# A Fourier and expert-mixing kernel on one core: the identity table loaded first, one product group per chunk, output products in quads over eight banks

## The chip, the cores and the metric

The kernel runs on one core of a Trainium2 chip. The metric is the device time of one execution in microseconds (us). The engines are named as in the profile: PE is the matrix engine (PEld its weight loads), DVE the vector engine, ACT the scalar engine, POOL the third elementwise engine, SP the engine that issues the transfers. PE's results land in PSUM, which has eight banks of 128 x 512 fp32; everything else lies in SBUF.

## The reference, cut to what matters

```python
X = np.fft.fft(np.fft.fft(x, axis=1), axis=2)      # x: 8 x 2496 x 256, fp32
x = X.real.reshape(8 * 2496, 256)                  # 19968 tokens
logits = x @ phi                                   # 32 slots, 8 experts x 4
d = np.exp(logits - logits.max(0)); d /= d.sum(0) + 1e-9
slot_input = d.T @ x                               # 32 x 256
for e in range(8):                                 # 4 slots each, F = 1024
    slot_out[e] = np.maximum(slot_input[e] @ w1[e], 0) @ w2[e]
c = np.exp(logits - logits.max(1, keepdims=True)); c /= c.sum(1, keepdims=True) + 1e-9
return c @ slot_out                                # 19968 x 256
```

## The kernel before, in words

The transformed tokens are never formed. The transform is linear, so the slots' table is transformed instead (`phi_`, `phv`), and the sequence's 2496 points are taken as 39 x 64. The eight sequences make five units: units 0 and 1 are one sequence each (two tiles of x), units 2 to 4 two sequences each (four tiles). A tile is 128 partitions of ten rows of 256 fp32, 1280 KB (1152 KB for the first tile of a two-sequence unit), and is loaded by `lx` into one of four buffers `raw`.

For each tile, `nf` adds the mirrored half (L349, mostly on POOL), `es` copies a half into PSUM (ACT) and `ef` writes sums and differences into a buffer `eo` (two DVE instructions, L365 and L366). Only then is the `raw` buffer free for the next load. Units 0 to 2 go on through PE: `pt` transposes against the identity (L379), `yt` copies the result out of PSUM into `xt`, and `zp` multiplies a chunk of ten rows by the slots' table (L410) in two groups, of four rows (128 columns) and of six (192 columns). Units 3 and 4 use DVE's 32 x 32 transpose (`xt`) and `zv` (L442) instead. Then, for each unit: `tz` (DVE transpose, L462), the 64-point product `am` (L482), the 39-point product `cm` (L503), the slots' maxima, the exponentials `xp`, the transform back (`em`, `dm`) and the product `um` with the kept `eo` tiles, which frees these for pieces of the weights (`lw`). When all units are done their sums are merged (`sl` to `si`), `hm` (L745) and `vm` (L779) apply the experts, and `rm`, `rc` make `rh`, the slots' outputs repeated on the four groups of 32 partitions.

The last stage makes the output. For each pair p of sequences a softmax over the slots (`x1` to `x6`) gives `hl`, and `om` multiplies 32 rows of `rh` by 32 rows of `hl`: five blocks b per pair, each with four row groups g, so 80 banks in all. Blocks 0 to 3 take one product of 512 columns for each g, block 4 two of 224. `oe` copies a bank into an output buffer (L907, ACT or DVE), and `st` stores a block of four banks (1024 KB, or 896 KB for block 4). In the trace every fp32 product is two MATMUL records, each with its weight load; transposes are one.

The order of the work is written out by hand in `ORDER`, a list of some 800 names such as `om.0.2.1`. Each engine, SP too, runs its instructions strictly in that order. PSUM banks and buffers are handed out in this order as well: `bank` takes the bank that was released first. The kernel before uses six banks this way; the other two hold `stage`, `ubank` and `mini` (maxima and sums).

Of the kernel before, what the change touches and what calls it, by code (L numbers as in the profile page):

```python
# [40 lines left out]
lx.3.1 am.0.1 tz.1.0.0 pt.2.0.2 es.2.2 nf.2.3.G cm_.0.0 ao.0.1.A ef.2.2.V yt.2.0.2.A pt.2.0.4 cm_.0.1
yt.2.0.4.A pt.2.0.3 mr.0.1 lx.3.2 lc_.0.0.A zp.2.0.0 mr.0.0 nf.3.0.G es.2.3 lc_.0.1.V cf.0.0 mt.0 pt.2.1.1
cf.0.1 yt.2.0.3.A ef.2.3.V pt.2.1.0 zp.2.0.1 yt.2.1.0.A mn.0 es.3.0 lx.3.3 pt.2.1.2 tz.1.0.1 nf.3.1.G pt.2.1.4
mw.0.A yt.2.1.1.A ef.3.0.V mb.0 pt.2.1.3 yt.2.1.2.A am.1.0 mq.0.A xp.0.0 tz.2.0.0 yt.2.1.4.A lx.4.0 phv xp.0.1
xt.3.0 yt.2.1.3.A nf.3.2.G es.3.1 zp.2.1.0 xp.0.4 ef.3.1.V am.1.1 ao.1.0.A zp.2.1.1 ao.1.1.A xp.0.3 xp.0.2
cm_.1.0 tz.2.0.1 lx.4.2 lw.17 xp.0.6 nf.3.3.G xp.0.5 tz.2.1.1 xp.0.7 cm_.1.1 xp.0.8 em.0.0 xp.0.9 tz.2.1.0
es.3.2 mr.1.0 am.2.1 xp.0.10 ec.0.0.A mr.1.1 nf.4.0.G xt.3.1 em.0.1 ao.2.1.A am.2.0 ec.0.1.A phw.A dm.0.0.0
ef.3.2.V mt.1 dc.0.0.0.A zv.3.0 ao.2.0.A mn.1 lx.4.1 es.3.3 xt.3.2 lc_.1.0.A mw.1.A ef.3.3.V dm.0.0.1 cm_.2.0
dc.0.0.1.A tz.3.0.0 cm_.2.1 lx.4.3 lc_.2.0.A xt.3.3 es.4.0 mb.1 am.2.2 um.0.0 nf.4.1.G ao.2.2.A mr.2.0 mq.1.A
lc_.2.1.A lc_.1.1.V cf.2.0 zv.3.1 mr.2.1 xp.1.0 xp.1.4 ef.4.0.V xp.1.8 cf.2.1 xp.1.3 xp.1.1 nf.4.2.G xp.1.10  # L50
xp.1.2 tz.3.0.1 xp.1.7 lw.6 lk.2 xp.1.6 tk.0 cm_.2.2 xp.1.5 tz.3.1.1 tc_.0.A xp.1.9 ct.0.0 es.4.1 tz.3.1.0
em.1.0 nf.4.3.G cc.0.0.A ef.4.1.V am.3.0 ec.1.0.A mr.2.2 lw.8 am.3.1 ao.3.0.A xt.4.0 es.4.2 em.1.1 mt.2
lc_.2.2.A cm_.3.0 ao.3.1.A ec.1.1.V cf.2.2 cf.1.0 cf.1.1 ef.4.2.V dm.1.0.0 am.3.2 dm.1.0.1 lc_.3.0.V lw.9
ao.3.2.A ct.0.1 es.4.3 mn.2 mr.3.0 cm_.3.2 dc.1.0.0.A uc.0.V cf.3.0 cm_.3.1 dc.1.0.1.A mw.2.V cc.0.1.V mb.2
ct.0.2 xt.4.1 mq.2.A um.1.0 xp.2.4 xp.2.8 xp.2.0 mr.3.2 xp.2.5 zv.4.0 xp.2.3 lw.3 lc_.3.2.V lc_.3.1.A ef.4.3.V
xp.2.9 xp.2.10 xp.2.2 xp.2.1 mr.3.1 lw.7 tk.1 em.2.0 xt.4.2 tc_.1.A cf.3.1 cf.3.2 xp.2.7 xp.2.6 mt.3 ec.2.0.A
em.2.1 mn.3 uc.1.A xt.4.3 mw.3.A em.2.2 ec.2.1.A dm.2.0.0 tz.4.0.0 ec.2.2.A mb.3 cc.0.2.A zv.4.1 tz.4.0.1
# [110 lines left out]
def _build(nc, tc, xh, phih, w1h, w2h, cins, where, out):  # L168
# [4 lines left out]
    with ctx:  # L173
# [228 lines left out]
        def zp(_, u, c, q):  # L402
# [11 lines left out]
            if q:  # L414
                drop(("et", u, c))
# [586 lines left out]
```

## Time and profile before

| what | value |
|---|---|
| median of 3 runs | 201.61 us (201.05 to 202.61) |
| the profiled execution | 200.02 us, span 198.2 us from first to last instruction |
[...]
| busy share of the span | PE 84%, PEld 56%, DVE 64%, ACT 47%, POOL 26% |
| moved by DMA | 59.15 MB, of these 20.45 MB written |

The busy time of PE counts records whose ends are modelled, so 84% isn't 84% of what it could do. A transfer is "issued" when SP hands it over and "landed" when its semaphore rises.

### The profile page before, as it was taken

The page shows a single profiled execution, that of the slowest core. Times are in us where ns is not written, and L with a number is a line of the kernel's source. Part 1 is how long each engine was busy: PE and PEld are TensorE (multiplying, and loading weights), DVE is VectorE, ACT ScalarE, POOL GpSimd, SP SyncE. Part 2 cuts the span into 40 slices and gives each one's busy share as a digit, 9 for nine tenths or more (in the row PEclk, how much of TensorE's full clock was granted, in tenths as well). Part 3 has the DMA queues.
Part 4 walks back from the last instruction along what each step waited for, and adds up shares of the span by engine and source line. Part 5 has one row for each costly group of instructions (what it writes and reads, how often), then busy time and mean ns, then how long its engine had stood idle before and what let it go on. Part 6 is the DMA issues. An engine that isn't in the chain of part 4 may idle for free.

```text
span 198.2 us, 5688 instructions
## 1 busy us (share of the span) xinstructions
PE 166.0 (84%) x2454; PEld 110.1 (56%) x2454; DVE 126.3 (64%) x209; ACT 93.1 (47%) x219; POOL 50.9 (26%) x35
## 2 busy tenths in 40 slices
PE   0006999884999998999999999989999989999920
PEld 0006887673755565667767875465456566756500
DVE  0753975980696995998938897999717532245420
ACT  0032637760664754786615642557645345421130
POOL 0046787879004920002000231006020000000000
PEclk9999999997999999999999999999999955555555
DMA  6999999899249398850089999402989998769865
GB/s 223 424 422 427 421 420 395 306 405 347 110 140 386 82 403 297 268 237 3 3 310 399 435 408 355 172 3 91 390 362 375 383 413 332 291 279 382 332 258 245
DMA packets 8952, 59.15 MB, mean 298 GB/s; under 512 B 1120, under 2 KB 1120, under 8 KB 4192
## 3 DMA queue, kind: packets, MB, share of 16 engines
q1 hardware_dynamic: 8928, 58.80, 75.3%
q8 instruction: 19, 0.31, 0.6%
q14 instruction: 5, 0.04, 0.1%
HBM read 38.35 MB, written 20.45 MB: 297 GB/s over the span
## 4 chain that ended last, share of the span: by engine, by line
PE 58%; DVE 4%; ACT 1%; issue 1%; ACTq 0%
PE psum L895 25%; PE psum L442 4%; PE psum L584 4%; PE psum L779 4%; PE psum L641 4%; PE psum L745 4%; PE psum L614 3%; PE psum L482 3%; PE psum L503 3%; PE psum L816 2%; DVE acc L697 1%; ACT raw L907 1%; DVE cm L861 1%; DVE es L601 1%; PE psum L800 0%
## 5 line engine op out<-in xcount | busy, mean ns | idle before, releaser
L349 POOL TENSOR_TENSOR raw<-raw 128x1280 f32<-128x1280 f32 (+1 forms) x14 | 39.0, 2794 | 30.5 <-DMA raw<-xh 18.1
L907 ACT COPY raw<-psum 128x512 f32<-128x512 f32 (+1 forms) x46 | 24.2, 587 | 29.7 <-PE psum L895 29.6
L907 DVE COPY raw<-psum 128x512 f32<-128x512 f32 (+1 forms) x34 | 21.6, 665 | 23.2 <-PE psum L895 23.0
L895 PE MATMUL psum<-ds,rh 32*128 32x512 f32 (+1 forms) x96 | 34.4, 748 | 0.6 <-ACT raw L907 0.6
L895 PE MATMUL psum<-es,rh 32*128 32x512 f32 (+1 forms) x96 | 30.9, 693 | 0.7 <-ACT rh L805 0.4
L379 PE MATMUL psum<-cs,eo 128*128 128x128 f32 x80 | 12.2, 302 | 16.5 <-DMA cs<-c 16.5
L895 PEld LDWEIGHTS psum<-ds,rh 32*128 32x128 f32 x96 | 18.3, 256 | 9.5 <-DVE raw L907 3.3
L895 PEld LDWEIGHTS psum<-es,rh 32*128 32x128 f32 x96 | 15.2, 235 | 9.4 <-ACT raw L907 3.8
L379 PEld LDWEIGHTS psum<-cs,eo 128*128 128x128 f32 x80 | 10.2, 157 | 18.0 <-issue 17.8
L462 DVE STREAM_TRANSPOSE zt<-psum 128x320 f32<-128x320 f32 x16 | 12.5, 836 | 10.0 <-PE psum L410 8.7
L574 ACT ACTIVATE d<-lt,nm 120x128 f32<-120x128 f32 (+1 forms) x55 | 16.5, 372 | 0.1
L365 DVE TENSOR_TENSOR eo<-raw,psum 128x640 f32<-128x640 f32 x15 | 12.1, 809 | 4.6 <-ACT psum L354 4.4
L410 PE MATMUL psum<-xt,wphi 128*32 128x128 f32 (+1 forms) x192 | 12.1, 317 | 3.2 <-issue 3.2
L354 ACT COPY psum<-raw 128x640 f32<-128x640 f32 x15 | 10.6, 705 | 6.8 <-POOL raw L349 6.2
L482 PE MATMUL psum<-cs,zt 128*64 128x64 f32 x352 | 13.2, 227 | 0.7 <-issue 0.7
L482 PEld LDWEIGHTS psum<-cs,zt 128*64 128x64 f32 x352 | 11.8, 141 | 2.5 <-issue 2.1
L584 PE MATMUL psum<-cs,d 120*64 120x60 f32 x352 | 12.2, 223 | 0.0
L584 PEld LDWEIGHTS psum<-cs,d 120*64 120x64 f32 x352 | 11.4, 138 | 1.4 <-issue 0.2
L366 DVE TENSOR_TENSOR eo<-raw,psum 128x640 f32<-128x640 f32 x15 | 12.1, 809 | 0.0
L495 ACT COPY o<-psum 124x512 f32<-124x512 f32 (+2 forms) x12 | 6.2, 524 | 12.2 <-PE psum L482 11.0
L423 DVE STREAM_TRANSPOSE xt<-eo 128x1280 f32<-128x1280 f32 x8 | 11.9, 1489 | 0.0
L387 ACT COPY xt<-psum 128x512 f32<-128x512 f32 x16 | 9.0, 589 | 6.2 <-PE psum L379 6.2
(129 smaller groups left out, 238.2 us busy)
## 6 DMA issues: line engine op xcount, KB each, us to landing
raw<-xh SPq DMA_DIRECT2D x13, 1280.0 KB, 7.5
out<-raw SPq DMA_DIRECT2D x15, 1024.0 KB, 4.7
eo<-w2h SPq DMA_DIRECT2D x12, 640.0 KB, 8.3
raw<-w1h SPq DMA_DIRECT2D x4, 1280.0 KB, 7.2
out<-raw SPq DMA_DIRECT2D x4, 896.0 KB, 4.0
raw<-xh SPq DMA_DIRECT2D x3, 1152.0 KB, 8.3
xt<-w1h SPq DMA_DIRECT2D x2, 1280.0 KB, 9.2
eo<-w1h SPq DMA_DIRECT2D x1, 512.0 KB, 3.6
```

What stands on the lines that cost most here:

```text
L349: (v if e == "V" else gp).tensor_tensor(a, a, b, op=ALU.add)
L365: en.tensor_tensor(b[:, :, 0:128], x[:, :, 0:128], y, op=ALU.add)
L366: en.tensor_tensor(b[:, :, 128:256], x[:, :, 0:128], y, op=ALU.subtract)
L379: pe.transpose(b[:, o : o + 128], T["eo", u, 2 * c + r // 5][:, r % 5, k * 128 : k * 128 + 128], C("ident"))
L410: pe.matmul(z[h][32 * g : 32 * g + 32, r0 : r0 + n], wphi[:, w], x[:, :, h, 32 * ah : 32 * ah + 32], start=i != 1, stop=i != 0, tile_posit ...
L423: v.transpose(T["xt", u, t // 2][:, 5 * (t % 2) : 5 * (t % 2) + 5].rearrange("p r n -> p (r n)"), T["eo", u, t].rearrange("p r d -> p (r d)"),
L462: v.transpose(dst, T["z", u, c][h])
L482: pe.matmul(ps[64 * r : 64 * r + 64, 64 * j : 64 * j + 64], T["zt", u][:, o : o + 64], C("wa0")[:, 64 * r : 64 * r + 64], start=True, stop ...
L574: sc.activation(d, src, AF.Exp, bias=nm[:, u % 2, i : i + 1], scale=1.0)
L584: pe.matmul(ps[64 * r : 64 * r + 64, 60 * j : 60 * j + 60], T["d", u, b][:120, 64 * j : 64 * j + 64], C(f"etab{r}"), start=True, stop=True ...
L895: pe.matmul(ps[:, j * w : j * w + w], rh[rows, 128 * dc : 128 * dc + 128], T["hl", p][rows, 32 * r0 : 32 * r0 + w], start=True, stop=True, ...
L907: COPY[e](T["ot", p, b][:, g * w : g * w + w], T["po", p, b, g][:, :w])
```

## The change

The tables are cut differently: the identity (64 KB) is a table of its own, transfer `lk.1`, and the other tables come behind it (`lk.2`, `lk.3`). The first tile of x is loaded as two pieces (two rows of each half, then three), with `nf` and `ef` in two pieces too. `zp` makes one group of 320 columns. `om` makes all four row groups of a block in one go, each in a bank of its own, and `rel`, run when the merging is done, gives the last two banks to the pool. `ini` clears `zt`'s padding once and runs one exponential. `rh` moves into a buffer `o1`. `ORDER` is rewritten throughout: among others `phv` moves from the middle of unit 2 to before the first `zp`, and one more `nf` runs on DVE. Operations `zq`, `zc` and a table `wq` are added for a kind of unit that isn't used.

```diff
@@ ORDER, its first and some of its last lines
-ini lx.0.0 lx.0.1 lx.1.0 lx.1.1 lk.1 lk.0 nf.0.0.V ef.0.0.V nf.0.1.V lx.2.0 es.0.1 ef.0.1.V nf.1.0.G lx.2.1
+ini lx.0.0.0.2 lx.0.1 lk.0 lk.1 nf.0.0.0.2.V lx.0.0.2.5 lx.1.0 lx.1.1 ef.0.0.0.2.V nf.0.1.V pt.0.0.0 phi_
...
-om.3.3.0 oe.2.3.3.V om.3.1.3 om.3.4.3 st.2.3.0.4 oe.3.4.0.V oe.3.1.3.V om.3.3.1 oe.3.4.3.V st.3.1.0.4 om.3.3.2
+om.2.4 oe.3.4.0.A oe.3.4.1.V oe.3.4.2.A oe.3.4.3.A oe.2.4.0.V om.3.3 st.3.4.0.4 oe.2.4.1.V oe.2.4.2.A
@@
+    unit = [("ident", np.eye(128))]
     zero = [
-        ("ident", np.eye(128)),
...
-    for group in (first, zero, late):
+    for group in (first, unit, zero, late):
@@
+        def more():
+            banks.extend([psum[:, 3072:3584], psum[:, 3584:4096]])
+            idle.extend([6, 7])
@@ lx
-        def lx(_, u, t):
+        def lx(_, u, t, a=0, b=0):
...
+            if b:
+                sy.dma_start(
+                    x.rearrange("p (m r) d -> p m r d", m=2)[:, :, a:b],
+                    xh[:, r0 * D : (r0 + 10) * D].rearrange("p (m r d) -> p m r d", m=2, d=D)[:, :, a:b],
+                )
+                return
@@ ini
+            gp.memset(sm[:, 39:40], 0.0)
+            sc.activation(sm[:, 39:40], sm[:, 39:40], AF.Exp)
             gp.memset(wphi[:, 1], 0.0)
+            for z in homes["zt"]:
+                gp.memset(z[:, 640:664], 0.0)
+                gp.memset(z[:, 1300:1324], 0.0)
@@ zp
-        ZR = ((0, 4), (4, 6))
-        def zp(_, u, c, q):
-            z = zbanks(u, c) if q == 0 else T["z", u, c]
-            r0, n = ZR[q]
+        def zp(_, u, c):
+            z = zbanks(u, c)
...
-                            z[h][32 * g : 32 * g + 32, r0 : r0 + n], wphi[:, w], x[:, :, h, 32 * ah : 32 * ah + 32],
+                            z[h][32 * g : 32 * g + 32], wphi[:, w], x[:, :, h, 32 * ah : 32 * ah + 32],
@@ rc
-            COPY[e](rh[:, 128 * dh : 128 * dh + 128], T["rm", dh][:, :128])
+            if dh == 0:
+                T["rh"] = home("rh", "o1")
+            COPY[e](T["rh"][:, 128 * dh : 128 * dh + 128], T["rm", dh][:, :128])
@@ om
+        def rel(_):
+            more()
-        def om(_, p, b, g):
-            ps = bank(("po", p, b, g))
-            T["po", p, b, g] = ps
-            rows = slice(32 * g, 32 * g + 32)
+        def om(_, p, b):
...
+            for g in range(4):
+                T["po", p, b, g] = bank(("po", p, b, g))
             for j, dc in enumerate(dcs):
+                for g in range(4):
+                    rows = slice(32 * g, 32 * g + 32)
+                    pe.matmul(
+                        T["po", p, b, g][:, j * w : j * w + w], T["rh"][rows, 128 * dc : 128 * dc + 128],
+                        T["hl", p][rows, 32 * r0 : 32 * r0 + w],
+                        start=True, stop=True, tile_position=(32 * g, 0),
+                    )
```

On SP at the start, before (`raw` are the four buffers of x, `c` and `phih` the tables; here the tables that hold the identity are `cs_98`):

```order
L267 DMA raw_61<-xh 128x2560
L267 DMA raw_62<-xh 128x2560
L267 DMA raw_63<-xh 128x2560
L267 DMA raw_64<-xh 128x2560
L256 DMA cs_98<-c 128x626
L253 DMA eo_65<-c 128x544
L254 DMA phi<-phih 128x64
L267 DMA raw_61<-xh 128x2304
```

and on SP at the start now (`cs_98` is the identity alone, `cs_99` the tables of the 64- and 39-point products):

```order
L272 DMA raw_61<-xh 128x2x512
L277 DMA raw_62<-xh 128x2560
L253 DMA eo_65<-c 128x544
L254 DMA phi<-phih 128x64
L256 DMA cs_98<-c 128x128
L272 DMA raw_61<-xh 128x2x768
L277 DMA raw_63<-xh 128x2560
L277 DMA raw_64<-xh 128x2560
L277 DMA raw_62<-xh 128x2304
L256 DMA cs_99<-c 128x498
```

The identity stood behind four whole tiles of x; now it stands behind one and two fifths of a tile, and the other tables behind five tiles.

On PE from unit 2's last chunk on, before (L410 is `zp`, L328 `phv`, L482 `am`):

```order
L410 MATMUL psum<-xt_79,wphi 32x192 x12
L379 MATMUL psum<-cs_98,eo_72 128x128 x2
L379 MATMUL psum<-cs_98,eo_73 128x128 x6
L554 MATMUL psum<-cs_98,mex 120x11
L379 MATMUL psum<-cs_98,eo_73 128x128 x4
L482 MATMUL psum<-cs_98,zt_86 64x64 x16
L328 MATMUL psum<-phi,eo_65 32x32 x72
L410 MATMUL psum<-xt_80,wphi 32x128 x12
L482 MATMUL psum<-cs_98,zt_86 64x64 x6
```

and on PE from its first instruction now (L405 is `pt`, L316 and L318 `phi_`, L350 `phv`, L431 `zp`, L531 `am`):

```order
L405 MATMUL psum<-cs_98,eo_66 128x128 x4
L316 MATMUL psum<-phi,eo_65 128x32 x4
L318 MATMUL psum<-phi,eo_65 1x32 x2
L405 MATMUL psum<-cs_98,eo_67 128x128 x8
L405 MATMUL psum<-cs_98,eo_66 128x128 x2
L405 MATMUL psum<-cs_98,eo_67 128x128 x2
L405 MATMUL psum<-cs_98,eo_66 128x128 x4
L350 MATMUL psum<-phi,eo_65 32x32 x72
L431 MATMUL psum<-xt_79,wphi 32x320 x12
L405 MATMUL psum<-cs_98,eo_68 128x128 x8
L531 MATMUL psum<-cs_99,zt_85 64x64 x22
```

The 72 small products of `phv` went from behind unit 1's second `am` to a place before the first `zp`, with only 26 PE products ahead of them.

On PE in the output stage, before (`es` and `ds` hold `hl` of the pairs, L895 is `om`):

```order
L895 MATMUL psum<-ds_90,rh 128x512
L895 MATMUL psum<-ds_90,rh 128x224 x2
L895 MATMUL psum<-ds_90,rh 128x512
L895 MATMUL psum<-es_87,rh 128x512
L895 MATMUL psum<-es_88,rh 128x512
L895 MATMUL psum<-es_88,rh 128x224 x2
L895 MATMUL psum<-es_88,rh 128x512 x2
L895 MATMUL psum<-es_87,rh 128x512
```

and on PE in the output stage now (`o_92` is `rh`, L952 is `om`):

```order
L952 MATMUL psum<-es_87,o_92 128x224 x8
L952 MATMUL psum<-es_87,o_92 128x512 x8
L952 MATMUL psum<-ds_90,o_92 128x512 x8
L952 MATMUL psum<-es_88,o_92 128x512 x4
L952 MATMUL psum<-ds_89,o_92 128x224 x8
L952 MATMUL psum<-ds_90,o_92 128x224 x8
```

Products of two or three blocks alternated, one row group at a time; now the four row groups of a block stand together.

## Rows read from the trace of the kernel before

**Rows 1.** The page, part 2: granted clock and DMA in 40 equal slices.
```profile
PEclk9999999997999999999999999999999955555555
DMA  6999999899249398850089999402989998769865
GB/s 223 424 422 427 421 420 395 306 405 347 110 140 386 82 403 297 268 237 3 3 310 399 435 408 355 172 3 91 390 362 375 383 413 332 291 279 382 332 258 245
```

**Rows 2.** Busy time by stretch; last three columns granted clock, DMA share, GB/s.
```profile
16.50:62.46 45.96, 41.27 (x719) 30.55 (x719) 32.72 (x48) 24.22 (x55) 27.38 (x17) 0.96 0.85 328
...
47.30:50.30 3.00, 3.00 (x30) 2.01 (x31) 0.00 (x0) 1.05 (x5) 2.45 (x3) 0.51 0.97 394
...
62.46:111.25 48.79, 48.07 (x1033) 33.55 (x1035) 39.02 (x66) 29.76 (x88) 10.37 (x7) 1.00 0.65 241
111.25:133.10 21.85, 21.06 (x388) 13.24 (x382) 19.36 (x42) 10.71 (x25) 3.52 (x3) 1.00 0.68 268
...
150.00:159.20 9.20, 8.64 (x48) 5.01 (x47) 5.15 (x9) 4.80 (x10) 0.00 (x0) 1.00 0.97 402
159.20:190.00 30.80, 30.05 (x92) 19.02 (x92) 12.53 (x20) 9.62 (x19) 0.00 (x0) 0.50 0.82 336
```

**Rows 3.** Timeline, the first 17 us: start, duration, engine, line; idle before in brackets.
```profile
6.35 1.49 DVE L349 TENSOR_TENSOR raw<-raw 128x1280 f32<-128x1280 f32 x1 [6.35 <-DMA raw<-xh]
...
16.50 4.27 PE L379 MATMUL psum<-cs,eo 128*128 128x128 f32 x24 [16.50 <-DMA cs<-c]
```

**Rows 4.** Timeline around PE's stop at 44 us.
```profile
41.81 1.40 PE L328 MATMUL psum<-phi,eo 128*32 128x32 f32 x142
...
47.28 1.08 PE L410 MATMUL psum<-xt,wphi 128*32 128x128 f32 x10 [3.21 <-issue]
...
51.26 1.51 DVE L462 STREAM_TRANSPOSE zt<-psum 128x320 f32<-128x320 f32 x2 [6.33 <-PE psum L410]
...
56.40 3.82 SPq L267 DMA_DIRECT2D raw<-xh  x2
```

**Rows 5.** Waits on SP's queue: total us, times, longest.
```profile
SPq L267 <- DVE eo L366: 48.6, 12, 11.3
```

**Rows 6.** DMA: instruction queue (packets, MB), bytes of the span, issues of x.
```profile
q8 instruction: 19, 0.31, 0.6%
...
HBM read 38.35 MB, written 20.45 MB: 297 GB/s over the span
...
raw<-xh SPq DMA_DIRECT2D x13, 1280.0 KB, 7.5
...
raw<-xh SPq DMA_DIRECT2D x3, 1152.0 KB, 8.3
```

**Rows 7.** The chain that ended last, in order of time: start, us, what.
```profile
64.81 2.82 PE psum L442 x72
...
102.92 1.70 PE psum L503 x4
...
127.48 1.72 PE psum L745 x16
...
133.12 4.79 PE psum L895 x21
...
159.20 15.54 PE psum L895 x37
```

**Rows 8.** Timeline: the two groups of unit 0's product.
```profile
22.92 1.10 PE L410 MATMUL psum<-xt,wphi 128*32 128x128 f32 x24
...
24.54 1.53 PE L410 MATMUL psum<-xt,wphi 128*32 128x192 f32 x24
```

**Rows 9.** Groups of instructions from 133 us on: busy us, mean ns, idle before.
```profile
L907 ACT COPY raw<-psum 128x512 f32<-128x512 f32 x39 | 21.4, 595 | 24.5 <-PE psum L895 24.4
...
L907 DVE COPY raw<-psum 128x512 f32<-128x512 f32 x25 | 16.5, 680 | 15.2 <-PE psum L895 15.1
```

**Rows 10.** Timeline of SP's queue: the stores.
```profile
136.60 54.95 SPq L913 DMA_DIRECT2D out<-raw  x22
```

More of the change, by code (lines that the diff above doesn't have):

```diff
@@ L41 @@
[L41 to L45, printed above, removed]
@@ L312, in phc @@
             v.tensor_copy(wphi[:1, 1], ps[:1, 32:64])
+            if any(f == "Q" for _, _, f in UNITS):
+                for k in range(2):
+                    v.tensor_copy(wq[:, k, 0], ps[:, 0:32])
+                    v.tensor_scalar(wq[:, k, 1], ps[:, 64:96], 1.0 - 2 * k, None, op0=ALU.mult)
+                    v.tensor_tensor(
+                        wq[:1, k, 0], wphi[:1, 0], ps[:1, 32:64], op=ALU.subtract if k else ALU.add
+                    )
             release("phi")
@@ L344, in nf @@
         @op
-        def nf(e, u, t):
-            lo = 1 if t == 0 and not single(u) else 0
+        def nf(e, u, t, r0=0, r1=5):
+            lo = first(u, t)
             x = T["x", u, t]
-            a, b = (x[:, 2:6], x[:, 6:10]) if lo else (x[:, 0:5], x[:, 5:10])
+            a, b = (x[:, 2:6], x[:, 6:10]) if lo else (x[:, r0:r1], x[:, 5 + r0 : 5 + r1])
             (v if e == "V" else gp).tensor_tensor(a, a, b, op=ALU.add)
@@ L352, in es @@
         def es(_, u, t):
-            lo = 1 if t == 0 and not single(u) else 0
+            lo = first(u, t)
             sc.copy(stage, T["x", u, t][:, lo : lo + 5, 128:256])
@@ L357, in ef @@
         @op
-        def ef(e, u, t):
-            lo = 1 if t == 0 and not single(u) else 0
-            x = T["x", u, t][:, lo : lo + 5]
-            b = home(("eo", u, t), "eo").rearrange("p (r d) -> p r d", d=D)
-            T["eo", u, t] = b
+        def ef(e, u, t, r0=0, r1=5):
+            lo = first(u, t)
+            x = T["x", u, t][:, lo + r0 : lo + r1]
+            if r0 == 0:
+                T["eo", u, t] = home(("eo", u, t), "eo").rearrange("p (r d) -> p r d", d=D)
+            b = T["eo", u, t][:, r0:r1]
             en = v if e == "V" else gp
@@ L366, in ef @@
             en.tensor_tensor(b[:, :, 128:256], x[:, :, 0:128], y, op=ALU.subtract)
[L367 removed]
+            if r1 == 5:
+                drop(("x", u, t))
         @op
@@ L903, in oe @@
             w = 512 if b < 4 else 448
-            if g == 0:
-                kind = next(k for k in OT if free[k])
-                T["ot", p, b] = home(("ot", p, b), kind)
+            if ("ot", p, b) not in T:
+                T["ot", p, b] = home(("ot", p, b), next(k for k in OT if free[k]))
             COPY[e](T["ot", p, b][:, g * w : g * w + w], T["po", p, b, g][:, :w])
```

158 lines of the change are left out of this document (91 added, 67 removed).

## The prediction

> **What bounds the kernel now.** I read the slices first. [...]
>
> The **input** begins with a wait. PE's first product starts at 16.50 us, released by the tables that hold the identity, although the first tile of x was there at 6.35 [rows 3]. Later PE stops for 3.21 us without any wait that the profile names, and this right after `phv`'s 142 records in 1.40 us [rows 4]; after it the clock is 0.51 for 3 us [rows 2]. DVE, strictly in order, then waits 6.33 us for `zp`, so that `ef` frees no buffer, and SP holds the next load of x for 11.3 us [rows 4, 5]. The last two tiles are issued at 56.4 and 59.9 us instead of a few us behind the others. In the **middle** the chain runs through PE from 62 to 111 us without a pause worth naming (48.07 of 48.79 us busy), with DVE at 39.02 of 48.79 behind it [rows 2]. From 111.25 to 133.1 the merging and the experts follow, one after the other. In the **output** PE is busy, ACT and DVE wait for it (24.4 and 15.1 us, [rows 9]), and the DMA stands at 0.97 only from 150 to 159 us; from 159.2, with the clock at half, it falls to 0.82 [rows 2]. There the bound is PE's own pace: 37 records in 15.54 us [rows 7].
>
> **The output stage.** A record of 512 columns that has the array to itself takes 1.70 / 4 = 0.43 us (`cm`). `hm`, whose four column groups follow each other in the program, makes 16 such records in 1.72 us, 0.11 each: four abreast. `om` before needs 4.79 / 21 = 0.23 us at the full clock and 15.54 / 37 = 0.42 at half [rows 7]: two abreast in both, since neighbours in the program often share a row group or wait for a bank. Quads put four different row groups and four banks side by side. If they run four abreast, a block of eight records takes 8 x 0.11 = 0.86 us, and 1.72 at the half clock; if only two abreast, 1.8 and 3.4 us. No row of before shows a quad of row groups; the nearest, `zv` (four row groups and two to four column groups), makes 72 records of 320 columns in 2.82 us, where alone each would take 0.43 x 320 / 512 = 0.27: nearly seven abreast. I take four abreast, and 3.4 us for the other end.
>
> Then the stores are late next. 20.45 MB are written [rows 6]; at the 402 GB/s of 150 to 159 us [rows 2] that is 50.9 us, or 2.6 us for each of 20 blocks, longer than the 1.72 of PE. Before, first `om` to the end took 198.2 - 133.1 = 65.1 us: 3.5 until the first store [rows 10], then a stream with holes. Now: 3.0 until the first store, 50.9, 1.9 for the last completion (the last store is issued at 191.55 [rows 10], and the last two, 1.9 MB, need 4.8 of the 6.7 us to the end), and 2.8 for holes while `vm`'s second half, the second `rc` and the softmax of pairs 1 and 3 share the engines. Sum 58.6, a gain of **6.5 us**; ends 0 (two abreast) and 9 (no holes).
>
> A copy takes 595 ns on ACT and 680 on DVE [rows 9]; two on each are 1.36 us a block, under the 2.6 of its store, while another block's banks are filled. [...]
>
> **The start and the input.** The stream begins at 6.35 minus one tile's 3.1 us (1.31 MB at about 422 GB/s), so at 3.2. Ahead of the identity now stand 512 + 1280 + 272 + 32 KB, with it 2160 KB or 2.21 MB: 5.2 us. PE can start at 8.4 instead of 16.5, 8 us earlier, with the first pieces' `nf` and `ef` done by then. This doesn't reach the end by itself, because x has to arrive: 13 x 1280 + 3 x 1152 KB [rows 6] are 20.6 MB, with the first tables and one piece of weights ahead of the last tile 21.9 MB, 52 us at 420 GB/s. If the queue never starves, the last tile is in at 55; before it came at about 64 (two tiles of 3.1 us behind issues at 56.4 and 59.9). The buffers decide that: four, each held for landing (7.5 us from issue), `nf`, `es`, `ef` and the wait for DVE, about 13 us in all, so 3.3 a tile against 3.1 of transfer. One `nf` less on POOL helps, 1.49 us more on DVE hurts.
>
> `phv`'s place matters. The instruction queue brings 0.31 MB in 19 packets [rows 6], about 63 bytes for each of PE's 4908 records, so I put the 3.21 us down to instructions used faster than they come: an inference, the row says only "issue". The 72 products take the same 1.40 us wherever they stand. Now only 26 products come before them, and at about 14 us; a stop there costs between nothing and 3.21 + 1.5 (half of 3 us at the half clock). In front of PE then lies work that waits for x anyway, and two tiles, 6 us, are queued in the DMA, so I take nothing; without that cover it would be 4.7.
>
> The single `zp` took 1.10 + 1.53 = 2.63 us in two groups [rows 8]. 24 records of 320 columns cost at least 24 x 2.82 / 72 = 0.94 and at most 2.63; PE's cost per column hardly falls from 128 to 192 (1.10 / 128 = 8.6 ns, 1.53 / 192 = 8.0), so I take 2.4, 0.2 saved in each of four chunks. What it loses is the early start: it waits for the last of five copies. The two cancel, within 1 us. The clearing of padding, the early exponential, `rh` in another buffer and the unused unit kind cost nothing: they lie before the first data or replace like by like.
>
> PE's work ahead of the second `zv` (at 64.81, [rows 7]) is about 43 us: 41.27 busy from 16.5 to 62.46 [rows 2] and 2 behind. From 8.4 it has 46 us until the last tile is in. So `zv` can start at 55 to 60; I take 57.8, **7 us** earlier, with ends 3 (the buffers hold x back as before) and 10. From there PE is the bound as before, the merging and the experts keep their 22 us, and the weights, whose `eo` buffers come free with `um`, move up with PE.
>
> **Sum.** 198.2 - 7.0 - 6.5 = 184.7 us of span, 186.5 with the 1.8 us around it (200.02 - 198.2). The median of before stands 0.8% above its profiled execution (201.61 / 200.02), which makes 188.0. I say 187, because the end of x reckoned from its bytes (55) is a little better than what I took.
>
> **The rivals.**
> First, x stays late, though PE starts early: DVE was busy 32.72 of the 45.96 us up to 62.46 although it stood 6.33 us for PE [rows 2, 4], and takes over an `nf`, the pieces and `wv`; if `ef` slips behind a transpose that waits for PE, the buffers come free no sooner. Then only the output gains: 198.2 - 6.5 + 1.8 = 193.5, on the median's scale 195. Against it: the 11.3 us hold had one cause, PE's stop.
>
> Second, the output keeps its length: a quad needs four banks at once, PE waits for four copies, the copies wait for PE, 1.72 + 1.36 + 0.3 = 3.4 us a block, or the quads run two abreast, also 3.4. 20 blocks make 67 us, no gain on 65.1. Only the 7 us are left: 193, or 194.5. Against it: eight banks hold two blocks.
>
> Third, more than I take: no holes and x in at 55, 198.2 - 10 - 9 + 1.8 = 181.
>
> Fourth, on the other side: the clock. [...] The 13.5 us of gain are gone after 27 us at the half clock; with 32 us it is 198.2 + 16 - 13.5 + 1.8 = 202.5, or 204. Against it: PE had gaps before 44 us too, with 41.27 of 45.96 us busy, and only slice 10 shows a lower clock [rows 1].
>
> **How the numbers follow.** Forecast 0.55; x late 0.14; output as long 0.13; more gain 0.07; both gains missing (200) 0.05; the clock 0.06. The range reaches from 180 to 196.5: it takes in the forecast with the ends of its two terms, the first two rivals and most of the third. A measurement of this kernel can tell about 1% from no change: faster 0.89, same 0.05, slower 0.06.
>
> **What would show it.** The first PE product at 8 to 9 us; loads of x without a hold over 5 us, the last issued by 52; the second `zv` at 55 to 60 and no PE stop over 2 us behind `phv` that DVE waits for; the clock at its upper level from 25 us to the output. In the output four records of `om` starting together, a block in 0.9 us (1.7 to 2.2 at half clock), DMA at 0.95 or more over the last 40 us, and PE now waiting for copies. Records of `om` two by two, a DMA share near 0.8, or ACT and DVE still waiting for PE would show the second term wrong; a hold of 8 us or more on SP would show the first wrong.

## The result, and the profile after

The changed kernel takes 188.5 us (median of 4 runs, 187.62 to 191.28), against 201.41 us for the kernel before on the same chip: a ratio of 0.9335, with an interval of 0.9276 to 0.9394. A run more than 1.5% above the fastest of its kernel counts as slow and is left out of the ratio: here that of 191.28 us, without which the median is 188.35. The prediction said 187.0, with a range of 180 to 196.5. The profiled execution took 188.35 us, 186.2 of them span. So the span fell by 12.0 us, where the sum had 13.5.

I compare the two traces at landmarks: the first product, the end of `zv` of unit 3, the first `hm`, the first `om`, the end.

| landmark, us of the span | before | after | difference |
|---|---|---|---|
| PE's first product | 16.50 | 8.88 | -7.6 |
| last load of x issued | 59.9 | 56.3 | -3.6 |
| end of the second `zv` | 67.6 | 62.6 | -5.0 |
| first `hm` | 121.2 | 118.0 | -3.2 |
| first `om` | 133.1 | 130.9 | -2.2 |
| end | 198.2 | 186.2 | -12.0 |

7.6 us are won at the start, but only 2.2 of them are left at the first `om`. The output stage gives the other 9.8: it lasted 65.1 us and now lasts 55.3. The slices of the page, part 2, say the same; they answer to [rows 1]:

```profile
PEclk9999999699999999999999999999999985978555
DMA  6999997899999568967994593930199999999994
GB/s 205 392 436 418 420 419 327 291 321 343 371 354 342 224 230 340 284 227 254 417 420 180 151 355 83 336 159 4 48 401 415 422 414 410 419 417 422 421 412 202
```

Of the last eleven slices all but the very last hold 401 to 422 GB/s, where before they went up and down between 258 and 413. In the input the hole at slices 11 and 12 is gone, yet slices 7 to 13 carry only 291 to 371. Ahead of the output the clock dips once, in slice 8. The windows of after, with the columns of [rows 2]:

```profile
8.88:28.70 19.82, 18.26 (x299) 14.45 (x301) 14.97 (x27) 8.15 (x15) 8.79 (x4) 1.00 1.02 422
28.70:32.54 3.84, 0.45 (x8) 0.00 (x0) 3.84 (x4) 0.84 (x3) 3.82 (x2) 0.97 0.75 311
32.54:57.00 24.46, 23.04 (x333) 15.91 (x339) 19.53 (x27) 16.96 (x44) 13.27 (x6) 0.94 0.92 339
...
118.11:130.91 12.80, 11.74 (x206) 5.86 (x198) 12.14 (x23) 6.06 (x16) 3.58 (x3) 1.00 0.38 141
...
133.50:150.00 16.50, 14.28 (x181) 7.58 (x174) 11.66 (x21) 10.86 (x23) 0.37 (x1) 1.00 0.97 391
150.00:178.80 28.80, 21.31 (x110) 11.91 (x108) 14.08 (x22) 15.33 (x31) 0.00 (x0) 0.71 1.01 416
```

The second row stands out: for 3.84 us PE does almost nothing (0.45 us busy), while DVE and POOL are busy throughout (3.84 and 3.82). In the last row PE has time to spare (21.31 of 28.80) at a mean clock of 0.71, and the DMA none. The timeline of after at the start answers to [rows 3, 4, 8]:

```profile
8.88 1.09 PE L405 MATMUL psum<-cs,eo 128*128 128x128 f32 x4 [8.88 <-DMA cs<-c]
...
15.31 1.43 PE L350 MATMUL psum<-phi,eo 128*32 128x32 f32 x144
...
16.64 2.38 PE L431 MATMUL psum<-xt,wphi 128*32 128x320 f32 x24
```

`phv` (L350) takes 1.43 us as before, and the next product follows with no stop. `zp` is one group of 2.38 us. The block at 28.7 us, in the timeline of after:

```profile
28.05 8.15 POOL L371 TENSOR_TENSOR raw<-raw 128x1280 f32<-128x1280 f32 x3 [0.47 <-DMA raw<-xh]
28.65 2.38 DVE L599 COPY mex<-mall 11x120 f32<-11x120 f32 x1
...
32.54 0.27 PE L603 MATMUL psum<-cs,mex 11*120 11x11 f32 x1 [3.39 <-DVE eo L389]
...
32.74 2.82 PE L405 MATMUL psum<-cs,eo 128*128 128x128 f32 x12
```

A copy of 11x120 (`mw`, which spreads a unit's maxima) holds DVE for 2.38 us and ends at 31.03. The first of POOL's three `nf` starts at 28.05, and one `nf` takes 2.9 us: it ends at 30.96. Behind the copy stand an `ef` (L388, L389), then PE's `mb` (L603), which waits for both. Behind PE's stop of 3.39 us the granted clock stands at 0.50 from 32.5 to 35.5 us, and the twelve transposes take 2.82 us. The `ef` frees a buffer, so SP's load waits as well, in the waits of SP's queue (compare [rows 5]):

```profile
SPq L277 <- DVE eo L389: 42.2, 11, 6.5
```

The longest hold is 6.5 us instead of 11.3. The chain that ended last, from the first `om` on (compare [rows 7]):

```profile
130.91 2.00 PE psum L952 x16
...
142.47 6.47 DMA out<-raw
...
154.14 3.42 PE psum L952 x32
...
158.77 7.35 DMA out<-raw
...
168.17 7.68 DMA out<-raw
```

Sixteen records of `om` take 2.00 us, 0.125 each, where before 21 took 4.79. The long pieces are now stores. The groups of instructions from 130 us on say who waits for whom (compare [rows 9]):

```profile
L963 ACT COPY raw<-psum 128x512 f32<-128x512 f32 x39 | 20.8, 594 | 12.8 <-DMA out<-raw 7.9 <-PE psum L952 4.8
...
L963 DVE COPY raw<-psum 128x512 f32<-128x512 f32 x25 | 16.3, 683 | 13.5 <-DMA out<-raw 8.0 <-PE psum L952 5.4
```

The copies take as long as before (594 and 683 ns), but wait mostly for a store to free their output buffer, and for PE 4.8 and 5.4 us instead of 24.4 and 15.1.

### The profile page after: what moved, and what is told of

Same layout as the page of the kernel before. It is cut to its first block, busy times and chain, and to the rows that moved or that the text cites. A ratio compares the mean times of both kernels' runs of the same rounds, so it can differ in the third digit from the quotient of the medians.

```text
span 186.2 us, 5489 instructions
## 1 busy us (share of the span) xinstructions
PE 149.6 (80%) x2358; PEld 97.6 (52%) x2358; DVE 129.2 (69%) x212; ACT 94.1 (51%) x222; POOL 44.2 (24%) x29
## 3 DMA queue, kind: packets, MB, share of 16 engines
HBM read 38.35 MB, written 20.45 MB: 316 GB/s over the span
## 4 chain that ended last, share of the span: by engine, by line
PE 48%; DMA 22%; DVE 15%; ACT 4%; issue 2%; SPq 2%; POOL 2%; ACTq 0%; DVEq 0%; POOLq 0%
DMA out<-raw 12%; DMA raw<-xh 11%; PE psum L633 6%; PE psum L496 6%; PE psum L690 5%; PE psum L663 5%; PE psum L552 5%; PE psum L952 4%; PE psum L531 4%; PE psum L405 3%; PE psum L867 3%; PE psum L431 2%; DVE eo L388 2%; DVE raw L963 2%; DVE eo L389 2%; ACT raw L963 2%
## 5 line engine op out<-in xcount | busy, mean ns | idle before, releaser
L371 POOL TENSOR_TENSOR raw<-raw 128x1280 f32<-128x1280 f32 (+1 forms) x13 | 36.0, 2787 | 30.0 <-DMA raw<-xh 25.5
L963 ACT COPY raw<-psum 128x512 f32<-128x512 f32 (+1 forms) x50 | 25.9, 582 | 17.9 <-DMA out<-raw 9.1
L963 DVE COPY raw<-psum 128x512 f32<-128x512 f32 (+1 forms) x30 | 19.3, 672 | 16.9 <-DMA out<-raw 9.1
L405 PE MATMUL psum<-cs,eo 128*128 128x128 f32 x80 | 14.2, 336 | 8.9 <-DMA cs<-c 8.9
L952 PE MATMUL psum<-es,o 32*128 32x512 f32 (+1 forms) x96 | 19.7, 650 | 2.0 <-ACT raw L963 1.1
L952 PE MATMUL psum<-ds,o 32*128 32x512 f32 (+1 forms) x96 | 16.2, 664 | 5.2 <-DVE ds L929 2.8
L405 PEld LDWEIGHTS psum<-cs,eo 128*128 128x128 f32 x80 | 11.7, 174 | 10.4 <-issue 9.4
L411 ACT COPY xt<-psum 128x512 f32<-128x512 f32 x16 | 8.9, 589 | 12.3 <-PE psum L405 12.2
L952 PEld LDWEIGHTS psum<-ds,o 32*128 32x128 f32 x96 | 8.8, 253 | 10.8 <-DVE raw L963 4.4
L952 PEld LDWEIGHTS psum<-es,o 32*128 32x128 f32 x96 | 9.1, 217 | 9.7 <-ACT raw L963 4.5
L388 DVE TENSOR_TENSOR eo<-raw,psum 128x640 f32<-128x640 f32 x14 | 11.4, 813 | 4.0 <-PE psum L704 1.1
L531 PE MATMUL psum<-cs,zt 128*64 128x64 f32 x352 | 12.2, 224 | 1.6 <-DMA cs<-c 1.6
L531 PEld LDWEIGHTS psum<-cs,zt 128*64 128x64 f32 x352 | 11.4, 138 | 2.7 <-DVE eo L388 1.8
L900 POOL TENSOR_TENSOR lt<-lt,cm 128x768 f32<-128x768 f32 (+1 forms) x3 | 4.0, 1337 | 36.7 <-PE psum L704 28.9
L552 PE MATMUL psum<-o,cs 124*120 124x512 f32 (+2 forms) x26 | 11.8, 553 | 1.0 <-ACT o L544 1.0
L477 DVE STREAM_TRANSPOSE xt<-eo 128x1280 f32<-128x1280 f32 x8 | 11.9, 1496 | 0.0
L389 DVE TENSOR_TENSOR eo<-raw,psum 128x640 f32<-128x640 f32 x14 | 11.4, 812 | 0.0
```

The source lines that it names most:

```text
L371: (v if e == "V" else gp).tensor_tensor(a, a, b, op=ALU.add)
L388: en.tensor_tensor(b[:, :, 0:128], x[:, :, 0:128], y, op=ALU.add)
L389: en.tensor_tensor(b[:, :, 128:256], x[:, :, 0:128], y, op=ALU.subtract)
L405: pe.transpose(b[:, o : o + 128], src[:, r % 5, k * 128 : k * 128 + 128], C("ident"))
L477: v.transpose(T["xt", u, t // 2][:, 5 * (t % 2) : 5 * (t % 2) + 5].rearrange("p r n -> p (r n)"), T["eo", u, t].rearrange("p r d -> p (r d)"),
L531: pe.matmul(ps[64 * r : 64 * r + 64, 64 * j : 64 * j + 64], T["zt", u][:, o : o + 64], C("wa0")[:, 64 * r : 64 * r + 64], start=True, stop ...
```

## The experiments

All times are medians of four runs; the kernel before took 200.83 to 201.42 us on the chips of these runs. Landmarks come from one trace of each kernel, and those ahead of the output vary between traces: with the same work ahead of it the first `om` stands at 133.1, 134.3 and 136.4 us in the three kernels with the old front, and at 130.9 and 132.5 in two with the new one. The stretch from the first `om` to the end is steadier: 55.3 to 55.5 us in eight traces with the changed output stage.

### What gave the output stage its gain

The change has two parts there: quads of row groups, and eight banks instead of six. Three runs, the kernel before and the changed kernel fill the table of two by two. First the kernel before with eight banks alone, its `om` single and in the old order:

```diff
- tk.4 x2.3.1.V hm.0.1 tc_.4.V sd x1.3.0 hm.1.0
+ tk.4 x2.3.1.V hm.0.1 tc_.4.V sd rel x1.3.0 hm.1.0
```

> The kernel before with the eight banks alone: the last two PSUM banks join the pool when the merging is done, the output products stay single and in the old order. Theory (neighbours that share a row group hold the products at two abreast, banks are no matter): 198.5 to 201.5, records of the output still about 0.42 us each at the half clock. Rival (the products waited for banks): DMA share 0.9 or more in the last 40 us, 191 to 195.

Measured: 194.33 us, ratio 0.969 (0.9661 to 0.9718). The first `om` stands at 134.33, in the chain of this kernel, and the span ends at 191.8: 57.5 us instead of 65.1.

```profile
134.33 4.00 PE psum L903 x21
```

My theory then, that neighbours of the same row group set the pace, fell, and the rival held: the same single records in the same order gained 7.6 us from two more banks. The DMA is nearly full now, in two windows of this kernel, where in windows of the same bounds before it stood at 0.96 and 0.73:

```profile
150.00:165.00 15.00, 14.36 (x77) 9.90 (x78) 7.33 (x12) 8.27 (x16) 0.00 (x0) 0.85 1.00 414
165.00:180.00 15.00, 15.00 (x58) 10.63 (x56) 7.58 (x13) 5.17 (x10) 0.00 (x0) 0.50 0.94 389
```

The copies still wait for PE, as the waits of this kernel show:

```profile
ACT raw L915 <- PE psum L903: 17.3, 14, 4.5
DVE raw L915 <- PE psum L903: 9.9, 10, 2.2
```

Then the kernel before with the whole new output stage, quads and eight banks (pairs 1 and 2 change places, as their softmaxes come in the other order there):

```diff
-        def om(_, p, b, g):
-            ps = bank(("po", p, b, g))
...
+        def om(_, p, b):
+            for g in range(4):
+                T["po", p, b, g] = bank(("po", p, b, g))
```

> The kernel before with the output stage of the changed one alone: quads of row groups over eight banks, blocks in the changed order with pairs 1 and 2 exchanged, since pair 1's softmax is done first here. Theory (the quads make the output bound by its stores): from the first output product to the end 55 to 57 us instead of 65, DMA share 0.95 or more from 140 us on, time 191 to 194. Rival (the output gained because the work in front left its engines free): 60 us or more, 196 to 200.

Measured: 193.34 us, ratio 0.9622 (0.9568 to 0.9676). From the first `om` at 136.43, in its chain, to the end at 192.7 are 56.3 us.

```profile
136.43 2.00 PE psum L899 x16
```

Its first `om` came 3.3 us later than the one in [rows 7], with the same work ahead of it (PE's stop behind `phv` took 4.38 us here, not 3.21), so the stretch tells more than the total. Here the copies wait for the stores, in its waits:

```profile
DVE raw L910 <- DMA out<-raw: 12.0, 9, 4.5
ACT raw L910 <- DMA out<-raw: 11.5, 9, 2.0
```

Last the changed kernel with six banks; an `om` is issued only where four banks are free. Of the moves that this takes the first are shown; others put the second half of `vm` and softmax steps ahead of the third quad:

```diff
- tc_.4.A sd rel x2.2.0.G
+ tc_.4.A sd x2.2.0.G
...
- om.0.2 x1.3.1 om.0.0 oe.0.2.0.A
+ om.0.2 x1.3.1 oe.0.2.0.A x2.3.1.G oe.0.2.1.V om.0.0
```

> The changed kernel with its quads of row groups, but with the six PSUM banks of the kernel before; a quad is issued only where four banks are free, so a few quads, copies and stores stand a little later. All work is done. Theory now: the two further banks carry most of the output's gain (with singles they alone took the stretch from the first om to the end from 65.1 to 57.5 us); with six banks a second quad can't start before two copies of the first are done, so PE and the copies take turns: 3 to 5 us more from the first om to the end (58 to 60 instead of 55.3), 191.5 to 193.5 us. Rival, that the quads by themselves make the gain, as the prediction had it (four abreast, stores the bound): the stretch stays at 55 to 56.5 us, time 188.5 to 189.5. Rival two, quads hurt without the banks: over 63 us for the stretch, over 196.

Measured: 191.57 us, ratio 0.9508 (0.9467 to 0.9549); the first `om` at 132.50, the end at 190.5: 58.0 us. The time fell where the theory had it, but its words "the banks carry most" are half the story, since quads on six banks are also 7.1 us better than singles on six. What the two missing banks, with the order that they ask for, cost lies at the beginning, in the chain of this kernel and in its windows (16.5 us from the first store on, as in the changed kernel's row from 133.50, and the 28.8 us behind):

```profile
132.50 3.10 PE psum L952 x16
```

```profile
135.10:151.60 16.50, 16.23 (x196) 9.88 (x194) 10.71 (x19) 10.34 (x22) 0.35 (x1) 1.00 0.80 321
151.60:180.40 28.80, 24.52 (x115) 14.28 (x112) 14.53 (x23) 14.72 (x29) 0.00 (x0) 0.70 0.99 409
```

The first sixteen records take 3.10 us, not 2.00, as the second quad finds only two free banks and stands behind two copies in the order; while the softmaxes and `vm` still share PE, the DMA moves 321 GB/s instead of 391. Behind that it moves 409 of 416, with six banks.

| first `om` to the end, us | six banks | eight banks |
|---|---|---|
| singles | 65.1 | 57.5 |
| quads | 58.0 | 55.3 (56.3 on the old input) |

Either part brings 7 to 8 us by itself, both together 9.8 (8.8 on the old input). The quads' 7.1 are read on the new input, so up to 1 us of them may be the input's, and with another order six banks might do better. The two don't add up, because the stores are the floor: 20.45 MB at the 416 GB/s of the last window are 49.2 us, and the first store is issued 2.6 us after the first `om`. With six banks the second quad waits for the copies that empty its banks (3.10 us for the first sixteen records against 2.00); with eight the copies wait mostly for the stores instead (7.9 and 8.0 us, for PE 4.8 and 5.4).

### What the early start is worth

The identity goes behind x's first five transfers again:

```diff
- ini lx.0.0.0.2 lx.0.1 lk.0 lk.1 nf.0.0.0.2.V lx.0.0.2.5 lx.1.0 lx.1.1 ef.0.0.0.2.V
+ ini lx.0.0.0.2 lx.0.1 nf.0.0.0.2.V lx.0.0.2.5 lx.1.0 lx.1.1 lk.1 lk.0 ef.0.0.0.2.V
```

> The changed kernel with the identity and the next tables loaded behind x's first five transfers again; all else as changed, all work done. Theory: PE starts some 6 us later (at 14 to 16 us), but behind the 20th us the input runs at the pace at which buffers come free and x arrives, so that only 1 to 3 us of it reach the end: 189.5 to 191.5 us. Rival one, PE's start was the whole of the front's gain and more: 6 to 7 us later all the way, 194 to 196. Rival two: nothing, since the front gained only 2.2 us before the output and other causes made that: 188 to 189.

Measured: 192.23 us, ratio 0.9528 (0.9495 to 0.9562), 3.7 us above the changed kernel, between the theory and its first rival. Its timeline shows why neither fits:

```profile
16.14 1.09 PE L405 MATMUL psum<-cs,eo 128*128 128x128 f32 x4 [16.14 <-DMA cs<-c]
...
34.94 0.21 DVE L599 COPY mex<-mall 11x120 f32<-11x120 f32 x1
```

PE starts 7.3 us later, but `mw` now falls beside no `nf` of POOL and takes 0.21 us instead of 2.38. So this kernel lacks the early start and also lacks the block at 28.7 us. Its first `om` stands at 134.75 in its chain; the next kernel, with the early start and without the block, has it at 128.5.

```profile
134.75 2.00 PE psum L952 x16
```

By these traces the early start is worth some 6 us, and the changed kernel, with its first `om` at 130.91, gave 2.4 of them back.

### The copy that held DVE

`mw` of unit 0 goes to ACT:

```diff
- nf.2.2.G mw.0.V lc_.0.0.A
+ nf.2.2.G mw.0.A lc_.0.0.A
```

> The changed kernel with one copy moved: the 11 x 120 copy `mw` of unit 0 runs on ACT, as before the change, and not on DVE, where it took 2.38 us and ended with POOL's `nf`. Theory (DVE is blocked by POOL in this copy, and PE's stop of 3.4 us at 29 us hangs on it): the copy takes 0.3 us, `ef` of the tile behind it starts 2 us earlier, PE's stop shrinks to about 1.5 us and SP's hold of 6.4 us to 4.4; the time falls by 1 to 3 us, 185.5 to 187.5. Rival (the arrival of x sets the pace, the stop is hidden behind it): the copy shrinks, the time stays, 188 to 189.

Measured: 185.96 us, ratio 0.9249 (0.9213 to 0.9286). One word in the order is worth about 2 us: 2.5 by the medians, 1.7 by the ratios (the two runs are not of the same chip, and the intervals overlap slightly), 2.4 at the first `om`. The timeline of this kernel:

```profile
28.77 0.29 ACT L599 COPY mex<-mall 11x120 f32<-11x120 f32 x1 [0.34 <-DVE mall L593]
...
30.35 0.19 PE L603 MATMUL psum<-cs,mex 11*120 11x11 f32 x1 [0.69 <-ACT lt L568]
...
30.47 1.53 PE L405 MATMUL psum<-cs,eo 128*128 128x128 f32 x12
```

PE's stop shrinks from 3.39 to 0.69 us, and SP's longest hold from 6.5 to 4.8. Behind the short stop the twelve transposes take 1.53 us instead of 2.82.

To see whether POOL was the cause I did the reverse elsewhere: in the changed kernel the `mw` of unit 2, which ran on ACT, goes to DVE beside another `nf`.

```diff
- nf.4.3.G mw.2.A am.3.1
+ nf.4.3.G mw.2.V am.3.1
```

> The changed kernel with the third unit's mw, a copy of 11x120, moved from ACT to DVE, where it stands beside a POOL product of 128x1280 (nf). The same work. Theory: such a copy on DVE doesn't get done while POOL's product runs, as the one of 2.38 us at 28.65 us that ended with POOL's nf: this one takes 1.5 to 3 us and ends with POOL's nf within 0.2 us; the time rises by 0 to 2.5 us (188.5 to 191). Rival: the 2.38 us had another cause (first use of that form, its place in PSUM): the moved copy takes 0.2 us as it did in the kernel before, and the time stays within 1 us of 188.5.

Measured: 189.67 us, ratio 0.9427 (0.9365 to 0.9489), 1.2 us above the changed kernel, with intervals that overlap; so the rows decide. In the timeline of this kernel:

```profile
61.67 5.79 POOL L371 TENSOR_TENSOR raw<-raw 128x1280 f32<-128x1280 f32 x2
...
65.94 1.59 DVE L599 COPY mex<-mall 11x120 f32<-11x120 f32 x1
```

The copy takes 1.59 us and ends at 67.53; POOL's second `nf` ends at 67.46. That is what the theory said, and the rival's 0.2 us is out. Over all runs the copy on DVE took 0.20 and 0.21 us with POOL idle, and 0.57 (in the run with `phv` in the middle) to 2.69 us beside an `nf`, according to how much of that was left.

### The order of `ef` and `mb`

`mb` and `mq` (maxima, L603 and its copy) use PSUM columns 3968 to 4096, `stage`, which `ef` reads, columns 3328 to 3968. They have the last bank in common, and in the program `mb` waits for the `ef` ahead of it. On top of `mw` on ACT, three `ef` now go behind the `mq`:

```diff
- mw.0.A lc_.0.0.A ef.2.1.V yt.2.0.1.A cf.0.0 mb.0 lc_.0.1.A mq.0.A cf.0.1
+ mw.0.A lc_.0.0.A yt.2.0.1.A cf.0.0 mb.0 lc_.0.1.A mq.0.A ef.2.1.V cf.0.1
...
- mb.2 uc.0.A ef.4.1.V dm.1.0.1 mq.2.A xp.2.4
+ mb.2 uc.0.A dm.1.0.1 mq.2.A ef.4.1.V xp.2.4
...
- mn.3 ef.4.3.V mw.3.A lc_.3.2.A lc_.3.1.A cf.3.2 mb.3 zv.4.0 cf.3.1 mq.3.V
+ mn.3 mw.3.A lc_.3.2.A lc_.3.1.A cf.3.2 mb.3 zv.4.0 cf.3.1 mq.3.V ef.4.3.V
```

> The previous kernel with three `ef` steps also put behind a step on the maxima: tile 1 of unit 2 behind `mq` of unit 0, tiles 1 and 3 of unit 4 behind `mq` of units 2 and 3. Theory (`mb` and `mq` wait for an `ef` that stands ahead of them in the list, because `mini` and `stage` share a PSUM bank): the stops of PE at 29, 69 and 83 us (3.8, 1.3 and 2.1 us between starts) all fall under 1 us and most of it reaches the end: 182.5 to 186. Rival (DVE is the real bound there and the stops only move): 186 to 189, with new stops of the same sum.

Measured: 184.55 us, ratio 0.9202 (0.9174 to 0.923). `mb` of unit 3 waited 1.82 us for `ef` in the changed kernel and in the one with `mw` on ACT; its row in the timeline of the changed kernel, and then of this one:

```profile
84.81 0.20 PE L603 MATMUL psum<-cs,mex 11*120 11x11 f32 x1 [1.82 <-DVE eo L389]
```

```profile
80.81 0.22 PE L603 MATMUL psum<-cs,mex 11*120 11x11 f32 x1
```

The wait is gone. The first of the three stops wasn't removed but moved: PE now waits for the `ef` at the transposes behind `mb`, which is over the 1 us of the expectation, and the nine transposes from 31.97 us on take 1.94 us, 0.22 each, where twelve took 0.13 each with `mw` on ACT:

```profile
31.24 0.33 PE L405 MATMUL psum<-cs,eo 128*128 128x128 f32 x1 [1.46 <-DVE eo L388]
...
127.00 2.00 PE L952 MATMUL psum<-es,o 32*128 32x512 f32 x16 [0.35 <-ACT o L856]
```

So the second `zv` ends later here than with `mw` on ACT alone (61.7 against 59.4 us), and yet the first `om` stands at 127.0 instead of 128.5. The time is 1.4 us lower on the same chip, with intervals that overlap; what is shown is that the waits at 69 and 83 us are gone.

### `phv` back in the middle

```diff
- pt.0.0.1 nf.1.0.V phv yt.0.0.2.V es.1.0
+ pt.0.0.1 nf.1.0.V yt.0.0.2.V es.1.0
...
- xp.0.9 am.1.1 yt.2.0.4.A
+ xp.0.9 am.1.1 phv yt.2.0.4.A
```

Its copies, `phw`, move behind it.

> The changed kernel with the 72 small products of phv behind the second em of the second chunk (am.1.1) again, some 30 us later than changed, and their copies behind that; the same work. Theory of the prediction, that PE's 3.21 us stop behind phv in the kernel before was instructions used faster than they come: a stop of 2 to 3.5 us with no named releaser within a few us behind phv, and, as PE is behind x there, 1 to 3.5 us more in the time (189.5 to 192). Rival, that the stop had to do with what stood behind phv in the kernel before and not with phv: no unnamed stop over 1 us behind it, 188 to 189.5.

Measured: 191.98 us, ratio 0.9505 (0.9457 to 0.9553), 3.5 us above the changed kernel (3.1 without the longest run of each). This isn't the price of the stop alone: `mw` was held for 0.57 us only, not 2.38, and the first `zp` took 4.42 us, not 2.38. The timeline (of an execution of 194.22 us, the longest of its four):

```profile
34.31 1.35 PE L350 MATMUL psum<-phi,eo 128*32 128x32 f32 x134
38.52 0.38 PE L350 MATMUL psum<-phi,eo 128*32 128x32 f32 x10 [2.86 <-issue]
```

The stop comes inside `phv`, after 134 of its 144 records, with no named releaser, and the clock is at 0.58 from 38.5 to 42.0 us. The traces of the kernel before and of the two with its front have the stop too, of 3.21, 3.32 and 4.38 us, behind `phv` and 14 records of `zp`. So the stop goes with `phv` in the middle, as the prediction inferred. That instructions run short is still an inference: 288 instructions (144 records, each with its weight load) of 63 bytes, the prediction's estimate, are 18 KB in 1.4 us, a little more than one packet of the instruction queue (19 for 0.31 MB [rows 6], 16 KB each). Why the same 144 records run through at 15 us, and at 23 in the run with the identity late, is not shown.

### The experts

From the first `hm` to the first `om` the kernel with the `ef` behind still needs 12.96 us, the kernel before 11.94. Its timeline shows a small product on DVE that took 0.17 us before, again beside a product of POOL:

```profile
116.27 0.89 DVE L780 TENSOR_TENSOR sm<-sm,tok 128x5 f32<-128x5 f32 x1 [0.33 <-ACT tok L712]
```

```profile
116.09 1.05 POOL L900 TENSOR_TENSOR lt<-lt,cm 128x512 f32<-128x512 f32 x1 [28.09 <-PE psum L704]
```

POOL ends at 117.14 us and DVE at 117.16. I moved that softmax product to DVE, and the sum behind it past the first transpose (`ht.0.0`):

```diff
- sd rel x2.2.0.G x1.2.1 hr.0.0.A hm.1.0 x3.2.0 ht.0.0 x2.2.1.G
+ sd rel x2.2.0.V hr.0.0.A hm.1.0 x3.2.0 ht.0.0 x1.2.1 x2.2.1.G
```

> The kernel x2 (mw on ACT, three ef behind the mq) with one softmax product of the third pair, x2.2.0, moved from POOL to DVE, and the reduction behind it on DVE moved behind the first transpose of the experts. All work done. In all kernels with the changed order of the middle the product sm<-sm,tok of 128x5 on DVE takes 884 to 886 ns beside that POOL product, where the kernels with the old order take 167 ns with POOL idle. Theory: DVE is held by POOL's product here too, though it is another instruction than the mw copy: it falls to 0.16 to 0.18 us; the chain behind it gains 0.2 to 0.7 us, the stage from the first hm to the first om is 12.3 to 12.8 us instead of 12.96, the time 183.9 to 184.6. Rival: the 0.88 us come from its operand tok, which ACT writes just before: the duration stays at 0.85 to 0.9 and the time at 184.55 within 0.6.

Measured: 184.79 us, ratio 0.9195 (0.9138 to 0.9251). The groups of this kernel (its L778 is the same line):

```profile
L778 DVE TENSOR_TENSOR sm<-sm,tok 128x5 f32<-128x5 f32 x1 | 0.2, 167 | 0.3 <-ACT tok L710 0.3
```

167 ns: POOL was the cause here too. But the stage got longer, not shorter: 13.70 us, since DVE now does POOL's work, and PE waits 1.1 us in all for its transposes, not 0.6. That part of the expectation failed, and the time is just above the 184.6 expected at most. Then the last transpose also ahead of a softmax chunk:

```diff
- vm.0.0.1 x4.2.1 hr.1.1.A cc.3.1.A vm.0.1.0 ht.1.1 x5.2.1.V
+ vm.0.0.1 hr.1.1.A cc.3.1.A vm.0.1.0 ht.1.1 x4.2.1 x5.2.1.V
```

> As x3_sm_free, and on DVE the last of the experts' transposes moved ahead of the sums and reciprocals of a softmax chunk (x4.2.1). All work done. Theory: what the experts' stage lost against the kernel before (12.96 against 11.94 us from the first hm to the first om) is DVE work that stands ahead of what PE waits for: the stage comes back to 11.9 to 12.2 us, the first om to 126.0 to 126.4, and 183.4 to 184.0 us of time. Rival: the softmax chunk that is now later holds the second half of the output's first blocks, the stretch from the first om to the end grows by as much, and the time stays at 184.5 within 0.5.

Measured: **183.81 us**, ratio 0.9133 (0.9097 to 0.9169), the fastest kernel of this study. The first `hm` (L792) and the first `om` (L950) in its timeline:

```profile
113.98 1.90 PE L792 MATMUL psum<-raw,sT 128*32 128x512 f32 x16
...
126.61 1.57 PE L950 MATMUL psum<-es,o 32*128 32x512 f32 x12 [0.35 <-ACT o L854]
```

12.63 us: the time came out as expected, but the stage regained a third of the 1.0 us lost, where the theory had it come back to 11.9 to 12.2 us. The rival, a longer stretch from the first `om` to the end, is out: 55.4 us as before. The time is 0.7 us below the kernel with the `ef` behind, measured on another chip; the two intervals just don't meet (0.9169 and 0.9174). The other 0.7 us of the stage stay open.

## Why the prediction was right, and where it was off

**The start** was right: PE begins at 8.88 us (8.4 forecast), and `phv` costs nothing early. Its 4.7 us without cover aren't tested: the run with `phv` in the middle is 3.1 to 3.5 us slower, but differs in `mw` and the first `zp` as well. `zp` takes 2.38 us (2.4). Of the clock rival 3 us came, not 27: the clock was at 0.50 from 32.5 to 35.5 us behind the stop in which `mw` has its part, so the sign "at its upper level from 25 us to the output" failed there. No run shows 27 or 32 us at the half clock in the input; what it costs shows in the twelve transposes, 2.82 us there and 1.53 with `mw` on ACT.

**The term of the front failed in size**: 7.0 us were forecast to reach the output, 2.2 did. The second `zv` ended 5.0 us earlier, inside the 3 to 10 that the term allowed, so 2.0 of the missing 4.8 were lost ahead of that and 2.8 behind. Wrong is the sentence that from there PE is the bound as before and "the merging and the experts keep their 22 us": from the end of `zv` to the first `om` took 65.5 us before and 68.3 after. The runs show where it went, and the prediction had none of it. `mw` on DVE beside POOL acts ahead of `zv`: on ACT the second `zv` ends at 59.4 us, 8.2 earlier than before, but the stretch behind it then takes 69.1 us, and 2.4 us arrive at the first `om`. `ef` ahead of `mb` makes PE wait behind `zv`: with three `ef` moved the stretch takes 65.3 us, as before, and 1.5 more arrive. From the first `hm` to the first `om` 1.0 us more are needed; 0.3 are regained by the order on DVE, and the cause of the rest is open. With the first two undone the first `om` stands at 127.0, 6.1 us earlier than before, which is nearly the 7 that were forecast; these sizes are of one trace each. The order shows the first two, and I read there only the places I had terms for. The last load of x went out at 56.3, not by 52, and the longest hold was 6.5 us, not under 5: that hold is SP's at the stop of 28.7 us, and with `mw` on ACT the second `zv` ends 3.2 us earlier.

**The term of the output was too small**: 6.5 forecast, 9.8 measured. The 58.6 us were 3.3 too long: 0.4 in the time to the first store (2.6, not 3.0), 1.7 in the rate (if all bytes are taken at the 416 GB/s of the last window, not at 402), and the rest, 1.2, in the holes and the last completion (3.5, not 4.7). The mechanism held as drawn: quads run nearly four abreast (0.125 us a record at the upper clock, where 0.11 was assumed and a lone one takes 0.43), the stores become the bound, the DMA stands at 0.97 and 1.01, and the copies wait. But I had put the gain on the quads alone and used the eight banks only as an argument against a rival; by the table above the banks alone give 7.6 of it.

So the total was close because the two errors, 4.8 us too much in front and 3.3 too little behind, lie on opposite sides. That part is luck.

## What to carry to other kernels

Ask of every instruction that changes its engine or its place which instruction of another engine now runs beside it, not only what it costs by itself: here a copy of 0.2 us became one of 2.4 and held DVE, PE and a load. When two remedies aim at the same stage, try each alone: quads and banks each won 7 to 8 us, both 9.8, and only the floor (bytes by rate) says how much is left. A gain at the start is worth what still stands at the last landmark; list the landmarks of both traces before explaining a total.

## What the runs showed of the hardware

- Two kinds of DVE instruction that read only SBUF were held while a POOL product ran, and ended with it, within 0.1 us: the copy of 11x120 took 1.59, 2.38 and 2.69 us instead of 0.20, the product of two tensors of 128x5 0.89 instead of 0.17. `ef`, one of whose operands is in PSUM, took 0.79 to 0.82 us beside the same `nf`. Nor was every instruction that reads only SBUF held: two transposes `xt` in the timeline of after, beside `nf` products that ran from 56.16 to 67.14 us, took 1.5 us each, as before. What holds the two kinds and not the others is not shown; still, I should have weighed what runs beside `mw`, since the diff moves it from ACT to DVE.
- In four traces PE stood for 2.9 to 4.4 us, with no named releaser, at or just behind 288 instructions that it took in some 1.4 us; at 15 us of the program the same ones ran through. That it had run out of instructions is an inference.
- Stores ran at 416 GB/s for 28.8 us with PE's mean clock at 0.71 and PE idle for 7.5 of them: there PE's clock isn't the bound any more.
